# High parts of v rounded on GpSimd, PSUM banks of the MLP exchanged, weight tiles spaced evenly

## The chip, the cores and the metric

The kernel runs on one core of one Trainium2 chip. The metric is the device time of one execution in microseconds. Each comparison rests on several executions; beside them one execution is recorded by the hardware profiler, and from that one come all rows and durations below.

## The reference

Attention with pooled queries, then two MLPs, all in float32:

```python
q_pool = q.reshape(B, H, S // 2, 2, D).mean(axis=3)          # B=2, H=8, S=1152, D=64
scores = (1 / sqrt(D)) * q_pool @ k.transpose(0, 1, 3, 2)
attn = softmax(scores)                                        # with 1e-9 in the denominator
x = (attn @ v)                                                # brought to 1152 tokens x 512
h = x @ w_in;  g = where(h > 0, h, exp(min(h, 0)) - 1);  x = g @ w_out      # 512 -> 2048 -> 512
h = x @ w2_in; g = h * tanh(softplus(h));                out = g @ w2_out   # 512 -> 2048 -> 512
```

The weights of both MLPs reach the kernel as 64-bit floats, two 32-bit words each, and are brought to float32 on the chip.

## The kernel before

**Precision.** TensorE multiplies numbers of reduced precision. So each operand is split into a high part, which is the rounded number, and a low part, the number minus its high part, and each product is made of two or three matmuls (high by high, high by low, low by high). A rounding is one copy to the type fp32r, the low part is one subtraction.

**Attention.** It goes through 8 pairs of heads, n = 0 to 7, each with 9 steps of 128 query rows. A step makes scores (`scores`, L331, into a `wide` tile of two PSUM banks and a part of the `rest` bank), maxima (L338, L341, VectorE), exponentials (L353, L355, ScalarE), nine transposes (`turn`, L386), and the split of the transposed probabilities. That split is done by ScalarE and VectorE (L411, L413) or, for 13 of 27 blocks in a pair, by ScalarE and GpSimd: ScalarE copies the block from PSUM to one of two `whole` buffers (L401), GpSimd makes the high part (L201) and the low part (L202). Then come the value matmuls (`values`, L426, into `psv` banks), and `join` (L439 on ScalarE, L441 on VectorE) brings their halves together into `xf`. `finish` scales by the reciprocals R, which go through DRAM (L374, L378), on GpSimd (L449) and splits the result (L451, L453) into `xh` and `xl`, the MLP's input.

**v.** In each pair `split_v` splits v in three parts of 128 x 384: the high part (L304) and the low part on GpSimd (L306). The key `vh` (`vl`) in the table `x` sets the place of each.

**Order.** In the attention the order on each engine is written out by hand: every operation has an event time, in steps, from the table `PP['x']`, and they are issued in the order of these times. The MLP's ScalarE and VectorE work is issued in the order of the program; TensorE's and SyncE's there is not.

**Weights.** A weight tile has a number j = 2i + a in each MLP: i is the block of 128 hidden units (0 to 15), a = 0 for w_in, a = 1 for w_out. To make a tile a raw load (L554 for w_in, L557 for w_out, into one of two `raw` buffers) and a chain of operations are needed: L574 on ScalarE, then L575, L576, L577 and L579 on VectorE. The float32 tile that comes out is either split at once (`parts`: L594 on ScalarE, L596 on VectorE or GpSimd) or saved to DRAM (L601) and read back later (L549), when only the split is left. 17 tiles of the first MLP are made and saved during the attention, at the times `cs0` to `cs16`, and j = 0 and 2 are made at `fs0` and `fs1`. The list `d1` names the tiles that are not among the 17; these are made on the spot in the MLP. Those of the second MLP in `c2` are made and saved in the step of the first MLP that the entry gives.

**MLP.** For each chunk of tokens 16 steps follow. up(s) is 12 matmuls (L733) into one of four `up` banks; `elu` or `mish` then makes `gh` and `gl` (in the first MLP L692 to L696). down(s), 12 matmuls (L753) into four `acc` banks, comes three steps after up(s). So TensorE's order is up(0), up(1), up(2), up(3), down(0), up(4), down(1) and so on. The weights of up(i) are asked for two steps ahead, those of down(i) at step i + 1.

**PSUM.** There are eight banks. The attention gives the first four to `wide` (pool `ps2`) and the last four to `ps1` and `rest` (pool `ps1`). The MLP's pools take their place in the order in which they are made: `accs` the first four, `ups` the last four.

**End.** `evac` copies each `acc` bank to SBUF (L769) and sends its rows out (L776).

Of the kernel before, what the change touches and what calls it, by code (L numbers as in the profile page):

```python
# [15 lines left out]
ALU = mybir.AluOpType  # L16
AX = mybir.AxisListType
PSUM = bass.MemoryType.PSUM
# [3 lines left out]
NT = B * SQ  # L22
DM = H * D
DFF = 2048
P = 128
# [14 lines left out]

PP = {
    'ma': 'pavgs',
    'd1': [4, 7, 10, 13, 16, 22, 28, 17, 1, 27, 2, 0],
    'c2': {'1': 15, '3': 13, '5': 18, '7': 19, '9': 20, '11': 25, '13': 22, '15': 21, '17': 24, '19': 24, '21': 26, '23': 27, '25': 28, '27': 29, '29': 29, '31': 31, '30': 17, '0': 30, '24': 30, '18': 7, '12': 6, '16': 11, '22': 17},
    'L': 3,
    'ng': 4,
# [66 lines left out]
    },  # L113
}

# [2 lines left out]
class Attention:  # L118
# [180 lines left out]
    def split_v(self, n, c, part):  # L299
        nc = self.nc  # L300
        x = self.rawv[n][:, :, 3 * c:3 * c + 3, :]
        hi, lo = (self.VS[n % 2][:, :, 3 * c:3 * c + 3, i, :] for i in range(2))
        if part == 0:
            nc.scalar.copy(hi, x)  # L304
        else:
            nc.gpsimd.tensor_tensor(lo, x, hi.bitcast(F32), op=ALU.subtract)  # L306

# [307 lines left out]
def build(ctx, tc, q, k, v, w1_in, w1_out, w2_in, w2_out, out):  # L615
    nc = tc.nc
# [49 lines left out]
        if key not in W.place:  # L666
            W.place[key] = [wpa.tile([P, DM], F32R, name="w%s%d_%d" % ((x,) + key)) for x in "hl"]
    wp, gp, tmp = pool("wp", 1), pool("gp", 1), pool("mtmp", PP.get('tb', 2))
    accs, ups = pool("accs", 8 - PP['upb'], space=PSUM), pool("ups", PP['upb'], space=PSUM)
    for key in need:  # L670
        if key not in W.place:
            W.place[key] = [wp.tile([P, DM], F32R, name="w%s%d_%d" % ((x,) + key)) for x in "hl"]
# [84 lines left out]
    def evac(m, c, u):  # L757
      with prio(PP['pe']):
        ps = acc[m, c][u]
        z0, z = Z[m][c]  # L760
        if m == 0:
            h, l = (x[:, u, z0:z0 + z] for x in (xh, xl))
            nc.scalar.copy(h, ps[:, :z])
            nc.vector.tensor_tensor(l, ps[:, :z], h.bitcast(F32), op=ALU.subtract)
            if u == NCC - 1:
                fresh_to[0] = z0 + z
        else:
            o = W.wt.tile([P, DM], F32, name="wt")
            nc.scalar.copy(o[:], ps[:])  # L769
            t, end = z0 + u * P, z0 + (u + 1) * P  # L770
            while t < end:
                b, r = divmod(t, SQ)
                j, p = divmod(r, PQ)
                n = min(PQ - p, end - t)
                x = t - z0 - u * P
                nc.sync.dma_start(rows[b, j, p:p + n], o[x:x + n, :])  # L776
                t += n

    L = PP['L']
# [66 lines left out]
```

## Time and profile before

| | us |
|---|---|
| three executions | 700.38, 700.95, 696.43 |
| their median | 700.38 |
| profiled execution, its own time | 698.07 |
| its span, first to last instruction | 696.3 |

The span is what the profile's rows divide up; the 1.8 us between it and the execution's own time lie around it. Times along the axis are counted from the start of the span: the attention goes to 278 us, the first MLP from there to about 493, the second to 691, and the output to the end. An engine that is busy for nearly all of a stretch need not be what bounds it, since in the attention several are; what counts is who waits for whom.

### The profile page before, as it was taken

The page shows a single profiled execution, that of the slowest core. Times are in us where ns is not written, and L with a number is a line of the kernel's source. Part 1 is how long each engine was busy: PE and PEld are TensorE (multiplying, and loading weights), DVE is VectorE, ACT ScalarE, POOL GpSimd, SP SyncE. Part 2 cuts the span into 40 slices and gives each one's busy share as a digit, 9 for nine tenths or more (in the row PEclk, how much of TensorE's full clock was granted, in tenths as well). Part 3 has the DMA queues.
Part 4 walks back from the last instruction along what each step waited for, and adds up shares of the span by engine and source line. Part 5 has one row for each costly group of instructions (what it writes and reads, how often), then busy time and mean ns, then how long its engine had stood idle before and what let it go on. Part 6 is the DMA issues. An engine that isn't in the chain of part 4 may idle for free. (4 is left out here: it accounts for less than half of the span.)

```text
span 696.3 us, 11828 instructions
## 1 busy us (share of the span) xinstructions
PE 668.4 (96%) x3995; PEld 608.2 (87%) x3995; DVE 600.5 (86%) x1111; ACT 475.1 (68%) x1125; POOL 263.8 (38%) x308
## 2 busy tenths in 40 slices
PE   7989999999989999799999999999989999999996
PEld 4888999989989998688888999999878999999995
DVE  4889999989999998889798877786999988888884
ACT  4989999989998998575655543666655464445443
POOL 2677888878787877152220000224130000000000
PEclk7999999999999999999999999999999999999999
DMA  6785866868586530646647667565120010001001
GB/s 173 200 206 155 214 190 175 222 160 212 176 211 160 154 109 31 212 139 199 209 137 205 188 195 211 152 194 177 42 76 16 0 47 1 0 1 47 0 1 45
DMA packets 66492, 91.24 MB, mean 131 GB/s; under 512 B 24376, under 2 KB 40832, under 8 KB 66432
## 3 DMA queue, kind: packets, MB, share of 16 engines
q1 hardware_dynamic: 66432, 90.50, 46.3%
q8 instruction: 31, 0.51, 0.3%
q14 instruction: 29, 0.24, 0.1%
HBM read 60.56 MB, written 12.88 MB: 105 GB/s over the span
## 5 line engine op out<-in xcount | busy, mean ns | idle before, releaser
L733 PE MATMUL up<-xh,wh 128*128 128x384 f32 (+2 forms) x384 | 129.7, 338 | 4.2 <-DVE xf L441 4.2
L596 POOL TENSOR_TENSOR wl<-wt,wh 128x512 fp32r<-128x512 f32 x38 | 50.9, 1354 | 208.5 <-ACT wh L594 180.2
L733 PE MATMUL up<-xh,wl 128*128 128x384 f32 (+2 forms) x384 | 129.9, 338 | 0.0
L733 PE MATMUL up<-xl,wh 128*128 128x384 f32 (+2 forms) x384 | 129.5, 337 | 0.0
L202 POOL TENSOR_TENSOR tl<-whole,th 128x384 fp32r<-128x384 f32 (+1 forms) x112 | 116.5, 1040 | 9.3
L386 PE MATMUL pst<-ident,a 128*128 128x128 f32 x648 | 102.9, 278 | 5.5 <-ACT a L355 2.8
L426 PE MATMUL psv<-th,vs 128*128 128x256 f32 (+1 forms) x288 | 86.9, 322 | 0.1
L386 PEld LDWEIGHTS pst<-ident,a 128*128 128x128 f32 x648 | 74.3, 141 | 14.2 <-ACT a L355 6.1
L733 PEld LDWEIGHTS up<-xh,wh 128*128 128x128 f32 x384 | 72.8, 190 | 9.1 <-issue 4.3
L426 PE MATMUL psv<-tl,vs 128*128 128x256 f32 (+1 forms) x288 | 79.3, 295 | 0.0
L341 DVE TENSOR_REDUCE neg<-wide 128x1 f32<-128x898 f32 x72 | 78.1, 1085 | 0.8
L355 ACT ACTIVATE a<-wide,neg 128x896 f32<-128x896 f32 x72 | 74.8, 1039 | 3.4 <-DVE neg L341 3.4
L733 PEld LDWEIGHTS up<-xl,wh 128*128 128x128 f32 x384 | 72.7, 189 | 4.7
L574 ACT ACTIVATE wt<-raw 128x512 f32<-128x512 f32 x64 | 43.9, 685 | 45.7 <-DMA raw<-in_moe_w_out_dram 28.6
L201 POOL TENSOR_SCALAR th<-whole 128x384 fp32r<-128x384 f32 (+1 forms) x112 | 58.9, 526 | 42.3 <-ACT whole L401 32.3
L733 PEld LDWEIGHTS up<-xh,wl 128*128 128x128 f32 x384 | 72.6, 189 | 2.6
L413 DVE TENSOR_TENSOR tl<-pst,th 128x384 fp32r<-128x384 f32 (+1 forms) x128 | 61.1, 500 | 10.5 <-ACT th L411 9.4
L706 ACT ACTIVATE e<-n 128x384 f32<-128x384 f32 x48 | 25.2, 526 | 65.3 <-DVE n L705 65.3
L331 PE MATMUL wide<-ks,qh 128*128 128x448 f32 (+1 forms) x160 | 62.3, 403 | 5.3 <-issue 3.8
L753 PE MATMUL acc<-gl,wh 128*128 128x512 f32 (+2 forms) x192 | 64.6, 337 | 0.9 <-DVE gl L696 0.9
L753 PE MATMUL acc<-gh,wh 128*128 128x512 f32 (+2 forms) x192 | 65.1, 339 | 0.1
L753 PE MATMUL acc<-gh,wl 128*128 128x512 f32 (+2 forms) x192 | 64.4, 336 | 0.0
(95 smaller groups left out, 1670.7 us busy)
## 6 DMA issues: line engine op xcount, KB each, us to landing
raw<-in_moe_w_out_dram SPq DMA_DIRECT2D x32, 512.0 KB, 4.4
raw<-in_moe_w_in_dram SPq DMA_DIRECT2D x32, 512.0 KB, 4.3
w<-wt SPq DMA_DIRECT2D x40, 256.0 KB, 4.2
wt<-w SPq DMA_DIRECT2D x40, 256.0 KB, 3.7
kr<-in_k_dram SPq DMA_DIRECT2D x16, 288.0 KB, 4.7
vr<-in_v_dram SPq DMA_DIRECT2D x8, 576.0 KB, 3.8
qr<-in_q_dram SPq DMA_DIRECT2D x7, 576.0 KB, 5.1
qh<-tqh SPq DMA_DIRECT2D x28, 144.0 KB, 2.8
```

What stands on the lines that cost most here:

```text
L201: nc.gpsimd.tensor_scalar(hi, x, 1.0, 1.0, op0=ALU.mult, op1=ALU.mult)
L202: nc.gpsimd.tensor_tensor(lo, x, hi.bitcast(F32), op=ALU.subtract)
L331: nc.tensor.matmul(dst, w[:], x[:, cols], start=(o == 0), stop=(o == len(ops) - 1))
L341: nc.vector.tensor_reduce(neg[:], wide[:, :, :WW + 1], axis=AX.XY, op=ALU.max, negate=True)
L355: nc.scalar.activation(a[:, :2 * WW].rearrange("p (c x) -> p c x", c=2), wide[:, :, :WW], AF.Exp, bias=neg[:], accum_out=self.sums[n][:, t ...
L386: nc.tensor.transpose(ps[:, i * P:(i + 1) * P], a[:, j * P:(j + 1) * P], self.ident[:])
L413: nc.vector.tensor_tensor(l, src[:, :, x0:x0 + w], h.bitcast(F32), op=ALU.subtract)
L426: nc.tensor.matmul(ps[:, :w], self.VS[n % 2][:, h, j].rearrange("p a d -> p (a d)"), t[:, j, :w], start=(c == 1), stop=(c == 2 * NKT))
L574: lambda: nc.scalar.activation(t[:], high.bitcast(F32), AF.Abs),
L596: e.tensor_tensor(l[:], t[:], h[:].bitcast(F32), op=ALU.subtract)
L733: nc.tensor.matmul(ps[:, :z], w, x, start=(o == 0), stop=(o == len(ops) - 1))
L753: nc.tensor.matmul(ps[:, :x.shape[1]], a, x, start=(i == 0 and o == 0), stop=(i == NFF - 1 and o == 2))
```

## The change

Four things are changed.

- The high part of v is made by GpSimd, as a multiplication by 1 (twice), in place of a copy on ScalarE. Its place in the order of events is the same, now on GpSimd's list.
- The two PSUM pools of the MLP are made in the other order: `ups` takes the first four banks, `accs` the last four.
- The list `d1` of tiles made on the spot is new. Before, the tiles made on the spot in the first MLP are j = 1, 4, 7, 10, 13, 16, 17, 22, 27, 28, and 29, 30 and 31, for which no place in the attention was left. After, they are 7, 9, 11, 14, 16, 18, 20, 22, 24, 26, 28, 30 and 31. Both are 13. The other 17 are made in the attention. The times of `cs4` and `cs16` are exchanged, so the tile that is made last there is j = 29 (before: j = 9); both are w_out tiles.
- The last output tile is copied in two halves, by ScalarE and VectorE, and the last of its two output transfers is issued by ScalarE.

The entry `isq` of the table only stands elsewhere in it.

```diff
-    'd1': [4, 7, 10, 13, 16, 22, 28, 17, 1, 27, 2, 0],
+    'd1': [7, 9, 11, 14, 16, 18, 20, 22, 24, 26, 28, 30, 31],
...
-        'cs2': 26.9397, 'cs3': 3.684, 'cs4': 76.2237, 'cs5': 22.2118, 'cs6': 35.9869, 'cs7': 9.0113, 'cs8': 49.2134, 'cs9': 58.2337, 'cs10': 44.9952,
-        'cs11': 31.1952, 'cs12': 62.3751, 'cs13': 7.9386, 'cs14': 40.1687, 'cs15': 13.2473, 'cs16': 53.9176, 'fs0': 66.983, 'fs1': 72.9632,
+        'cs2': 26.9397, 'cs3': 3.684, 'cs4': 53.9176, 'cs5': 22.2118, 'cs6': 35.9869, 'cs7': 9.0113, 'cs8': 49.2134, 'cs9': 58.2337, 'cs10': 44.9952,
+        'cs11': 31.1952, 'cs12': 62.3751, 'cs13': 7.9386, 'cs14': 40.1687, 'cs15': 13.2473, 'cs16': 76.2237, 'fs0': 66.983, 'fs1': 72.9632,
...
         hi, lo = (self.VS[n % 2][:, :, 3 * c:3 * c + 3, i, :] for i in range(2))
         if part == 0:
-            nc.scalar.copy(hi, x)
+            nc.gpsimd.tensor_scalar(hi, x, 1.0, 1.0, op0=ALU.mult, op1=ALU.mult)
         else:
             nc.gpsimd.tensor_tensor(lo, x, hi.bitcast(F32), op=ALU.subtract)
...
-    accs, ups = pool("accs", 8 - PP['upb'], space=PSUM), pool("ups", PP['upb'], space=PSUM)
+    ups, accs = pool("ups", PP['upb'], space=PSUM), pool("accs", 8 - PP['upb'], space=PSUM)
...
             o = W.wt.tile([P, DM], F32, name="wt")
-            nc.scalar.copy(o[:], ps[:])
+            last = z0 + (u + 1) * P == NT
+            if last:
+                nc.scalar.copy(o[:, :DM // 2], ps[:, :DM // 2])
+                nc.vector.tensor_copy(o[:, DM // 2:], ps[:, DM // 2:])
+            else:
+                nc.scalar.copy(o[:], ps[:])
...
-                nc.sync.dma_start(rows[b, j, p:p + n], o[x:x + n, :])
+                (nc.scalar if last and end - t == n else nc.sync).dma_start(rows[b, j, p:p + n], o[x:x + n, :])
```

## Rows read from the trace of the kernel before

**Rows 1.** The page, part 2: granted TensorE clock in 40 slices, in tenths.

```profile
PEclk7999999999999999999999999999999999999999
```

**Rows 2.** Stages: length, busy us (instructions) of PE PEld DVE ACT POOL, clock, DMA.

```profile
36.00:270.00 234.00, 224.64 (x1618) 210.63 (x1617) 219.46 (x396) 219.38 (x580) 189.39 (x232) 1.00 0.66 173
...
278.30:282.60 4.30, 0.14 (x2) 0.03 (x1) 4.11 (x9) 1.30 (x3) 0.00 (x0) 1.00 0.47 138
282.60:286.20 3.60, 3.60 (x9) 2.81 (x10) 2.46 (x3) 0.87 (x2) 1.43 (x1) 0.56 0.98 333
...
312.00:332.00 20.00, 20.00 (x90) 16.57 (x89) 18.28 (x31) 11.83 (x23) 4.54 (x3) 1.00 0.62 197
```

**Rows 3.** Timeline of TensorE from attention to MLP: start, duration, line, [idle before <-releaser].

```profile
278.16 0.28 PE L426 MATMUL psv<-tl,vs 128*128 128x256 f32 x1
282.60 0.47 PE L733 MATMUL up<-xh,wh 128*128 128x512 f32 x1 [4.16 <-DVE xf L441]
...
295.19 0.39 PE L753 MATMUL acc<-gh,wh 128*128 128x512 f32 x1
```

**Rows 4.** Timeline of VectorE and ScalarE in the same stretch.

```profile
282.49 0.69 DVE L596 TENSOR_TENSOR wl<-wt,wh 128x512 fp32r<-128x512 f32 x1
283.56 0.69 ACT L574 ACTIVATE wt<-raw 128x512 f32<-128x512 f32 x1 [3.69 <-DMA raw<-in_moe_w_in_dram]
293.25 0.68 DVE L696 TENSOR_TENSOR gl<-up,gh 128x512 fp32r<-128x512 f32 x1
```

**Rows 5.** Timeline of TensorE at the start of a pair's scores.

```profile
143.48 0.47 PE L331 MATMUL wide<-ks,qh 128*128 128x448 f32 x1 [1.51 <-DMA ks<-kl]
```

**Rows 6.** Line L549, read-back of saved tiles: issue to landing.

```profile
DMA to landing us min/median/max: 2.5/3.7/5.4
```

**Rows 7.** Groups by line, 36 to 270 us: busy us, mean ns | idle before.

```profile
L201 POOL TENSOR_SCALAR th<-whole 128x384 fp32r<-128x384 f32 x87 | 47.6, 547 | 25.9 <-ACT whole L401 16.0 <-ACT row L372 8.2 <-PE pst L386 1.4
L413 DVE TENSOR_TENSOR tl<-pst,th 128x384 fp32r<-128x384 f32 x87 | 46.3, 550 | 6.7 <-ACT th L411 5.8
L331 PE MATMUL wide<-ks,qh 128*128 128x448 f32 x72 | 30.3, 436 | 5.3 <-issue 3.8 <-DMA ks<-kl 1.5
L304 ACT CAST vs<-vr 128x384 fp32r<-128x384 f32 x19 | 10.6, 559 | 0.0
```

**Rows 8.** Timeline of ScalarE and VectorE in a pair without a wait for keys.

```profile
106.78 0.59 ACT L304 CAST vs<-vr 128x384 fp32r<-128x384 f32 x1
107.78 1.02 DVE L413 TENSOR_TENSOR tl<-pst,th 128x384 fp32r<-128x384 f32 x2 [0.41 <-ACT th L411]
```

**Rows 9.** Timeline of GpSimd and ScalarE in the same pair.

```profile
103.20 0.35 POOL L201 TENSOR_SCALAR th<-whole 128x192 fp32r<-128x192 f32 x1 [1.31 <-ACT whole L401]
110.39 1.37 POOL L202 TENSOR_TENSOR tl<-whole,th 128x384 fp32r<-128x384 f32 x1
112.22 0.49 ACT L401 COPY whole<-pst 128x384 f32<-128x384 f32 x1
```

**Rows 10.** Timeline of VectorE: one operation without and with GpSimd at work.

```profile
291.00 0.42 DVE L575 TENSOR_SCALAR wt<-wt 128x512 f32<-128x512 f32 x1
301.87 1.05 DVE L575 TENSOR_SCALAR wt<-wt 128x512 f32<-128x512 f32 x1
```

**Rows 11.** Timeline of ScalarE, VectorE and TensorE in steps 6 to 9.

```profile
316.53 0.67 ACT L574 ACTIVATE wt<-raw 128x512 f32<-128x512 f32 x1 [2.71 <-DMA raw<-in_moe_w_out_dram]
321.03 0.66 ACT L574 ACTIVATE wt<-raw 128x512 f32<-128x512 f32 x1 [3.32 <-DMA raw<-in_moe_w_in_dram]
321.73 0.43 DVE L575 TENSOR_SCALAR wt<-wt 128x512 f32<-128x512 f32 x1 [1.04 <-ACT wt L574]
323.98 0.68 DVE L696 TENSOR_TENSOR gl<-up,gh 128x512 fp32r<-128x512 f32 x1
327.83 0.39 PE L753 MATMUL acc<-gh,wh 128*128 128x512 f32 x1
```

**Rows 12.** Timeline of SyncE at the end: six issues.

```profile
690.25 3.08 SPq L776 DMA_DIRECT2D out_dram<-wt  x6
```

42 rows, old and new, of the table PP are left out of this document.

## The prediction

> **What bounds the kernel now.** I read the page first, then busy time by stage, then the single stages along the time axis, then the groups of instructions. The page shows TensorE at the full clock in all 40 slices but the first [rows 1]. The stages show what slices of 17 us hide [rows 2]. From 36 to 270 us, the steady attention, TensorE, VectorE and ScalarE are all at 94 to 96% and GpSimd at 81% (189.4 of 234): three engines share the bound there. In the MLP (312 to 332) TensorE never pauses, 90 matmuls in 20.0 us, so there only a late operand costs time. [...] The rows of the hole name its end: the last attention matmul starts at 278.16, the first up-matmul at 282.60 after a wait for the xf addition of VectorE (L441), the last reader of an attention bank [rows 3]. The first down-matmul, down(0), starts at 295.19. Four up steps of 12 matmuls lie before it; at some 0.226 us each (20.0/90 = 0.222, a little more as the window's edges cut matmuls) that is 10.9 us, so of the 16.9 us from 278.3 to 295.2 some 6.0 are lost: 4.3 idle and about 1.7 by the slow clock.
>
> **Banks exchanged.** After the change the up tiles lie where the score tiles lay. These are last read by the exponentials, before the last transposes and value matmuls of the attention, so up(0) may follow the value matmuls at 278.3 at once. What is late next is the weights. For j=2 (up(1)) the low part is the subtraction at 282.49, done at 283.18 [rows 4]; VectorE works without a pause up to it, so it doesn't come sooner. up(1) needs it in its third matmul, at 278.3 + 14 x 0.226 = 281.5: a wait of 1.7 us. In the attention TensorE waits 1.51 us at one place [rows 5] in a stretch whose clock stays at 1.00 [rows 2], so I count no slow stretch behind it. Tile j=4 (up(2), due at 283.2 + 10 x 0.226 = 285.5) is no longer made on the spot, where its first step waited 3.69 us for a load and ran at 283.56 [rows 4]; it is read back, 3.7 us from issue to landing [rows 6]. Issued at about 279.3, in the place of the load that it replaces, it lands at 283 and is split by 284.5: in time. Tile j=1 likewise. down(0) also needs gl(0), which came at 293.25 + 0.68 because two made-on-the-spot chains stood before it on ScalarE and VectorE [rows 4]; both are gone, and by 290.9 it is there. So down(0) starts at 278.3 + 10.9 + 1.7 = 290.9 instead of 295.2: a gain of 4.3 us. Bounds: 6.0 if nothing is late, 0 if something holds down(0) until 295. As TensorE has no pause in the stretch behind it, the gain stays.
>
> **v on GpSimd.** 24 casts (8 pairs, 3 parts) of 559 ns leave ScalarE, 13.4 us, and 24 operations like the 547 ns of L201 come to GpSimd, 13.1 us [rows 7]; the trace has no such operation on v itself, but L201 has its shape and form. GpSimd goes from 81 to about 86% in the steady stretch. Bounds: a gain of 13.4 us if ScalarE alone set the pace, a loss of 13.1 if GpSimd did. The nearest rows lie close to neither. Behind the cast at 106.78, VectorE waits 0.41 us for ScalarE [rows 8]; that wait can go. But GpSimd works without a pause from 103.20 past 112, and the split that ends at 110.39 + 1.37 = 111.76 frees the buffer that ScalarE fills at 112.22, 0.46 us later [rows 9]. Two new operations fall into this stretch, 1.1 us, so that copy would wait about 0.64 us, with the exponentials and casts of ScalarE queued behind it, and VectorE, which has no slack there, behind these. In the pairs where TensorE waits before the scores (L331, 5.3 us in the stretch, the longest for the keys' DMA [rows 5, 7]), that wait covers GpSimd's delay, and the gain on ScalarE is mostly swallowed by it too. I count +0.4 us in each of three pairs without that wait and -0.3 in four with it: 0 in sum. At the start nothing moves: the three casts of the first pair follow the parts that the first scores need.
>
> The other side of the edit is VectorE. The same operation on SBUF alone, L575, takes 0.42 us with GpSimd idle and 1.05 with it at work [rows 10]. GpSimd's busy share rises by 13.1/234 = 5.6%, so only that share of VectorE's SBUF-only work meets it anew, and most of VectorE's attention work reads PSUM; under 1 us, counted at nothing. [...]
>
> **Weight tiles.** Thirteen tiles are made on the spot before and after. Before, they start at j=4 and 1, in the hole; after, the first is j=7, and j=7, 14, 9, 16, 11 and 18, with two tiles of the second MLP (c2 entries 12 and 18), fall to steps 4 to 7: 8 chains where there were 5. Each chain is about 2.25 us of VectorE (321.73 to 323.98) and holds one of two load buffers, and ScalarE stands still until its load has landed: 3.32 us at 321.03, with four chains in steps 6 and 7. The gl(6) that this delays is done at 323.98 + 0.68; its down starts at 327.83, so 3.2 us of slack were left [rows 11]. In the new order step 6 has three chains, the third loaded only when the first has freed its buffer. By the same rows (one chain per 4.5 us, 316.53 to 321.03 on ScalarE) the high parts of j=16 and 18 come within a us of their ups. I count a loss of 1.0 us; bounds 0 (the slack of 3.2 holds) and 8 (8 chains x 4.5 = 36 us against four steps of 24 x 0.226 = 5.4 and some 6 us of slack). Exchanging cs4 and cs16 keeps the tile that is saved last a w_out tile, so nothing moves.
>
> **The end.** Six output DMAs are issued on SyncE in 3.08 us, 0.51 each [rows 12]. Now one is issued by ScalarE beside SyncE's five, after two half copies: the last issue on SyncE ends 0.5 us sooner. Gain 0.5.
>
> **Sum.** -4.3 + 0 + 1.0 - 0.5 = -3.8. Against the profiled execution's own 698.07 (span 696.3, 1.8 around it): 694.3. The three runs have their median at 700.38, 2.3 above; the middle of all four is 699.2, and the forecast on it is 695.4, 0.7% under the median.
>
> **Rivals.** (1) ScalarE held the attention back and GpSimd isn't late: VectorE's waits for the casts, 5.8 us at L413 [rows 7], go: 689.6. Against: VectorE is as full as ScalarE. Chance 0.25. (2) The exchange brings nothing forward, as read-back tiles land late or down(0) is held otherwise: the 4.3 go, 699.7. For it: all read-backs share SyncE with the transfer of R; chance 0.15. (3) Bunched weight tiles stall TensorE in steps 7 to 10 by the bound of 8 us: 702.4. For it: ScalarE's standing in rows 11; against: the slack of 3.2 us there. 0.17. (4) The other side: GpSimd becomes the bound of the attention. It decides once GpSimd's stretch outlasts its idle time in each pair, and each new operation then costs its full 0.55: 695.4 + 13.1 = 708.5, slower. Against: 1.31 us of idle time ahead of the stretch [rows 9], and 19% overall. 0.08. (5) Each new operation blocks one of VectorE's SBUF-only ones: 24 x 0.63 = 15.1, 710.5. Against: these are a small part of its work, and GpSimd meets them now. 0.04. The forecast keeps 0.31, its own range being 692 to 699.
>
> **Chances.** About 1% is what a measurement of this kernel can tell from no change: 693.4 and 707.4. Faster: most of (1), 0.21, and a quarter of the forecast, 0.08. Slower: most of (4), (5) and a worse (3), 0.09. The rest, 0.62, is within 1%. The range, 688 to 703, takes in the forecast, (2), (3) and (1) with up to 1.6 us more; (4), (5) and the far ends of (1) and (3) are left out.
>
> **What would show it.** First up-matmul within 0.3 us of the last value matmul, no clock under 0.9 in the 4 us after, one wait of about 1.7 us in up(1), down(0) 12 to 13 us after the last value matmul. In the attention: the time from pair to pair unchanged within 0.5 us; ScalarE waiting for GpSimd at L401 by 0.5 us and more in some pairs. In steps 8 to 10, ups that wait up to 1 us for wl. The prediction is wrong if the attention's end moves by over 3 us, if down(0) still starts 16 us after it, or if the waits in the MLP sum to over 6 us more than now.

## The result, and the profile after

The changed kernel is slower by 0.67%: a ratio of 1.0067 to the kernel before, with a 95% interval of 1.0043 to 1.0090 (medians 703.49 and 699.23 us of runs on the same chip). That is within the 1% of the forecast's middle class, but the forecast was 0.7% faster, and 703.5 lies just above its range. The profiled execution took 703.30 us with a span of 701.26, to be set beside 698.07 and 696.28.

Four times cut both spans into stages: the last value matmul, down(0), the first up of the second MLP, and the end of the last matmul.

| Stage | before, us | after, us | difference |
|---|---|---|---|
| start to last value matmul (attention) | 278.16 | 282.79 | +4.6 |
| to down(0) (transition) | 17.03 | 12.49 | -4.5 |
| to the first up of the second MLP | 187.12 | 192.64 | +5.5 |
| to the end of the last matmul | 208.65 | 208.59 | -0.1 |
| to the end of the span | 5.32 | 4.75 | -0.6 |

So the gain at the transition came as forecast, and two losses hid it. The transition first, in the timeline of TensorE (columns as in [rows 3]):

```profile
282.79 0.28 PE L426 MATMUL psv<-tl,vs 128*128 128x256 f32 x1
282.91 0.39 PE L733 MATMUL up<-xh,wh 128*128 128x512 f32 x1
...
286.16 0.39 PE L733 MATMUL up<-xh,wh 128*128 128x512 f32 x1
...
287.87 0.50 PE L733 MATMUL up<-xh,wl 128*128 128x512 f32 x1 [1.09 <-DVE wl L596]
...
295.28 0.39 PE L753 MATMUL acc<-gh,wh 128*128 128x512 f32 x1
```

The wait of 4.16 us for the attention's last VectorE operation [rows 3], the hole from 278.3 to 282.6 us, is gone: the first up-matmul follows at once. One wait is left, 1.09 us for the low part of j=2. The forecast had 1.7 us at the third matmul of up(1). In this kernel TensorE does two more matmuls with high parts first (the third starts at 286.16), so only the fifth waits; the low part itself is as late as forecast (287.87 less 286.16 is 1.7). The stages, with the columns of [rows 2], show that the clock no longer falls there (1.00 from 282.9 to 287.5 us, where 0.56 was granted behind the hole [rows 2]), what the steady attention looks like, and the new hole in the MLP:

```profile
36.00:270.00 234.00, 221.28 (x1582) 205.93 (x1581) 216.10 (x387) 209.46 (x549) 194.55 (x245) 1.00 0.66 173
282.90:287.50 4.60, 3.88 (x18) 2.75 (x16) 4.41 (x9) 3.34 (x7) 0.00 (x0) 1.00 0.67 233
...
316.00:336.00 20.00, 16.94 (x71) 12.66 (x70) 16.72 (x28) 12.26 (x23) 4.28 (x3) 1.00 0.69 205
```

In 20 us of the MLP TensorE does 71 matmuls where it did 90 [rows 2]. What it waits for from the transition into the second MLP, in the list of waits (engine, tile and line, releaser: us in total, times, longest):

```profile
PE up L733 <- DVE wl L596: 3.5, 3, 1.4
PE acc L753 <- ACT gh L712: 1.7, 1, 1.7
PE up L733 <- ACT wh L594: 1.3, 2, 1.1
PE acc L753 <- DVE xl L764: 1.0, 2, 0.6
PE up L733 <- POOL wl L596: 0.6, 1, 0.6
```

The three lines of "up" are new. Apart from the 1.09 us at up(1), which the first of them holds, they are weight tiles that come late at up(8), up(9) and up(15). Read as lengthened distances from one matmul to the next, the places of over 0.3 us in that stage sum to 5.8 us here (0.4 to 1.5 each) and to 1.0 in the kernel before. The line with gh, in the second MLP, is in the kernel before too, at the same 1.7 us.

In the attention, ScalarE is freed as meant, from 219.4 to 209.5 us in the steady stretch, and GpSimd goes from 189.4 to 194.6. The groups by line and shape (columns of [rows 7]) show the price of the cast in its new place; the last fence has the narrower shape of L413 in the kernel before:

```profile
L413 DVE TENSOR_TENSOR tl<-pst,th 128x384 fp32r<-128x384 f32 x84 | 44.9, 546 | 6.6 <-ACT th L411 6.2
...
L304 POOL TENSOR_SCALAR vs<-vr 128x384 fp32r<-128x384 f32 x19 | 14.6, 768 | 0.0
L413 DVE TENSOR_TENSOR tl<-pst,th 128x192 fp32r<-128x192 f32 x28 | 8.6, 352 | 2.6 <-ACT th L411 2.5
```

```profile
L413 DVE TENSOR_TENSOR tl<-pst,th 128x192 fp32r<-128x192 f32 x28 | 8.6, 351 | 1.1 <-ACT th L411 1.0
```

A cast of v takes 768 ns on GpSimd in this stretch, not the 547 that the forecast took from L201. VectorE's wait for ScalarE's casts at L413, which was to shrink, is 6.2 us where it was 5.8 [rows 7], and for the narrower shape 2.5 where it was 1.0. The timeline shows how, in the pair that answers to [rows 8, 9]:

```profile
111.70 0.72 DVE L579 SCALAR_TENSOR_TENSOR wt<-raw,wt 128x512 int32<-128x512 int32 x1
111.84 0.95 POOL L304 TENSOR_SCALAR vs<-vr 128x384 fp32r<-128x384 f32 x1
113.35 1.01 POOL L202 TENSOR_TENSOR tl<-whole,th 128x384 fp32r<-128x384 f32 x1
114.40 0.48 ACT L401 COPY whole<-pst 128x384 f32<-128x384 f32 x1 [0.49 <-POOL tl L202]
115.75 0.56 DVE L413 TENSOR_TENSOR tl<-pst,th 128x384 fp32r<-128x384 f32 x1 [0.48 <-ACT th L411]
```

The cast at 111.84 lasts 0.95 us, beside VectorE's L579. The split behind it ends at 114.36 and only then may ScalarE refill the buffer `whole`: it waited 0.49 us, with the exponentials queued behind, and VectorE's next subtraction waited 0.48.

### The profile page after: what moved, and what is told of

The parts are those of the page before. It is cut to its first block, busy times and chain, and to the rows that moved or that the text cites. A ratio compares the mean times of both kernels' runs of the same rounds, so it can differ in the third digit from the quotient of the medians.

```text
span 701.3 us, 11837 instructions
## 1 busy us (share of the span) xinstructions
PE 670.4 (96%) x3995; PEld 606.7 (87%) x3995; DVE 604.6 (86%) x1112; ACT 467.3 (67%) x1101; POOL 275.0 (39%) x332
## 5 line engine op out<-in xcount | busy, mean ns | idle before, releaser
L201 POOL TENSOR_SCALAR th<-whole 128x384 fp32r<-128x384 f32 (+1 forms) x112 | 58.3, 521 | 38.1 <-ACT whole L401 30.6
L413 DVE TENSOR_TENSOR tl<-pst,th 128x384 fp32r<-128x384 f32 (+1 forms) x128 | 61.2, 498 | 11.7 <-ACT th L411 11.2
```

Of the source, the lines that this page charges most:

```text
L201: nc.gpsimd.tensor_scalar(hi, x, 1.0, 1.0, op0=ALU.mult, op1=ALU.mult)
L413: nc.vector.tensor_tensor(l, src[:, :, x0:x0 + w], h.bitcast(F32), op=ALU.subtract)
```

## Each part alone

The first four runs undo or do one part at a time. In the edits below the kernel before is the base unless something else is said.

**v alone.**

```diff
-            nc.scalar.copy(hi, x)
+            nc.gpsimd.tensor_scalar(hi, x, 1.0, 1.0, op0=ALU.mult, op1=ALU.mult)
```

> The kernel before with one edit: the high parts of v on GpSimd. Theory A (ScalarE's copies into the buffers `whole` wait for GpSimd): the attention alone loses what it lost in the changed kernel, its last value matmul at about 282.8 instead of 278.2, pairs that don't wait for the keys' DMA 32.4 us apart instead of 31.5, and the time is 4 to 5 us over the kernel before (about 703.5). Rival B (the other order of the saved weight tiles, which also run through the attention, did it): last value matmul within 0.7 us of 278.2, no difference in time.

**Banks alone.**

```diff
-    accs, ups = pool("accs", 8 - PP['upb'], space=PSUM), pool("ups", PP['upb'], space=PSUM)
+    ups, accs = pool("ups", PP['upb'], space=PSUM), pool("accs", 8 - PP['upb'], space=PSUM)
```

> The kernel before with one edit: the PSUM banks of the MLP exchanged, the weight tiles as before (j=4 and j=1 still made on the spot in the hole). Theory C (the exchange and the tiles are worth their 4.5 us only together): up(0) follows the last value matmul at once, but up(2) waits for j=4 and down(0) for gl(0), which stand behind two made-on-the-spot chains; down(0) starts 14 to 16 us after the last value matmul instead of 17.0, a gain of 1 to 3 us. Rival D (the banks alone bring the gain): down(0) 12.5 us after it, gain 4.5 us, 694.7.

**Tiles alone.**

```diff
-    'd1': [4, 7, 10, 13, 16, 22, 28, 17, 1, 27, 2, 0],
+    'd1': [7, 9, 11, 14, 16, 18, 20, 22, 24, 26, 28, 30, 31],
-        'cs4': 76.2237, ... 'cs16': 53.9176
+        'cs4': 53.9176, ... 'cs16': 76.2237
```

> The kernel before with one edit: the list of the tiles made on the spot (and cs4 with cs16 exchanged). Theory E (the bunching in steps 4 to 7 is what stalls TensorE): the stalls of steps 8 to 16, 5.5 us in the changed kernel, are there in full although nothing brings TensorE forward; time up by 4 to 5 us. Rival F (the stalls are the gain of the transition handed back, the chains can't follow a TensorE that is 4.5 us earlier): stalls under 2 us, and the time within 2 us of the kernel before.

**All but v.** The changed kernel with `nc.scalar.copy(hi, x)` back in its place.

> The changed kernel with one edit undone: the high parts of v are back on ScalarE; banks, tiles and the end as changed. By theory A the attention ends at 278.2 as in the kernel before, down(0) starts 12.5 us later at 290.7, the stalls of steps 8 to 16 stay at about 5.5 us, and the time is 0 to 1 us over the kernel before (699 to 700), 4.6 under the changed one. By rival B the attention still ends at 282.8 and the time is that of the changed kernel (703.5).

| Run | ratio to before (95%) | attention ends | down(0) after it | first up of the second MLP after it |
|---|---|---|---|---|
| before | | 278.2 | 17.0 | 204.2 |
| changed | 1.0067 (1.0043 to 1.0090) | 282.8 | 12.5 | 205.1 |
| v alone | 1.0046 (1.0022 to 1.0069) | 282.0 | 17.0 | 203.1 |
| banks alone | 1.0004 (0.9984 to 1.0024) | 276.1 | 17.8 | 203.3 |
| tiles alone | 1.0094 (1.0071 to 1.0118) | 277.0 | 17.7 | 211.0 |
| all but v | 1.0018 (0.9988 to 1.0048) | 280.6 | 12.5 | 205.0 |

The end of the attention differs from execution to execution (275.0 to 280.9 us in the twelve profiled executions with v on ScalarE, as the waits for transfers at the start of the pairs differ), so one trace doesn't price v; the timed ratios and the pairs do. The 280.6 of all but v, for one, holds a wait of 2.67 us for the keys and a clock of 0.57 in the 4 us behind it.

*v alone* costs 0.46%, 3.2 us, less than the 4 to 5 of theory A, but where it said: the weight tiles have no part in the attention's loss. From the first scores of a pair to those of the next, the third and fourth pair, which don't wait for the keys, take 32.45 and 32.55 us instead of 31.51 and 31.60. The last pair takes 38.87 us from its first scores to the last value matmul instead of 37.82, and in the twelve executions with v on ScalarE this is 37.77 to 37.83.

*Banks alone* bring nothing. Rival D falls; theory C had the reason, but its gain of 1 to 3 us didn't come. up(0) starts at once, but up(1) waits 1.54 us and up(2) 2.71, the latter for j=4, which is still made on the spot, and behind that the clock is down, so that down(0) comes 17.8 us after the attention:

```profile
281.19 0.50 PE L733 MATMUL up<-xh,wl 128*128 128x512 f32 x1 [1.54 <-DVE wl L596]
...
286.46 0.50 PE L733 MATMUL up<-xh,wh 128*128 128x512 f32 x1 [2.71 <-ACT wh L594]
```

```profile
281.20:283.60 2.40, 2.40 (x10) 1.78 (x10) 1.25 (x2) 1.78 (x3) 1.08 (x1) 1.00 0.92 292
286.40:290.00 3.60, 3.54 (x11) 2.50 (x12) 3.46 (x7) 2.61 (x6) 0.00 (x0) 0.74 0.75 247
290.00:294.00 4.00, 4.00 (x16) 3.27 (x15) 3.18 (x5) 3.26 (x7) 2.04 (x2) 0.80 0.72 239
```

(The second fence has stages around the two waits; the clock is the third number from the end: 1.00, 0.74, 0.80.) *Tiles alone* cost 0.94%, 6.6 us (theory E had 4 to 5), though nothing brings TensorE forward, and the same late tiles stand in its list of waits:

```profile
PE up L733 <- DVE wl L596: 2.5, 2, 1.6
PE up L733 <- ACT wh L594: 1.2, 2, 0.8
PE up L733 <- POOL wl L596: 0.6, 1, 0.6
```

So theory E holds against F: the stalls belong to the list. Banks and tiles are worth their gain only together: 0.3 and 6.6 us alone, 1.3 together (with the halved last output), 5.6 less than their sum. And v's 3.2 and the 1.3 make 4.5 of the measured 4.7 us.

## Where v's loss comes from

If it is the place in GpSimd's order, another place must mend it. In the run with v alone GpSimd was idle for 0.9 us just before buffer 14 of each pair, and busy without a pause from there to the last part of v.

```diff
-        'vh0': 7.0318, ... 'vh2': 6.5211,
+        'vh0': 5.31, ... 'vh2': 5.3,
```

> The kernel before with v on GpSimd, and the casts of two of its three parts (vh0 and vh2) moved to an earlier place of GpSimd's order, before the `whole` buffer number 14 of a pair, where the run with v on GpSimd shows GpSimd idle for 0.9 us. Theory A (the place matters: the casts lie in the stretch in which GpSimd has no pause, and make ScalarE's copies wait for it at L401): the pairs, less the waits for the keys, are 31.4 to 31.7 us apart again and the last pair 37.8 instead of 38.9; the time is 2.5 to 3.5 us under that run, within 1 us of the kernel before. [...]

The ratio is 1.0008 (0.9978 to 1.0037), no loss that can be told from zero. Its interval still overlaps that of v alone (1.0022 to 1.0069) a little, so the times by themselves don't settle it. The traces do, for theory A: the last pair takes 37.93 us, where casts that cost the same at any place would have left it at the 38.87 of v alone. The two traces at the same place, the turn from pair 6 to pair 7 (GpSimd, VectorE and ScalarE), first with v at its old place, then early:

```profile
240.17 0.51 POOL L304 TENSOR_SCALAR vs<-vr 128x384 fp32r<-128x384 f32 x1
243.06 0.73 DVE L579 SCALAR_TENSOR_TENSOR wt<-raw,wt 128x512 int32<-128x512 int32 x1
243.18 0.98 POOL L304 TENSOR_SCALAR vs<-vr 128x384 fp32r<-128x384 f32 x1
245.79 0.48 ACT L401 COPY whole<-pst 128x384 f32<-128x384 f32 x1 [0.52 <-POOL tl L202]
```

```profile
230.92 1.20 POOL L304 TENSOR_SCALAR vs<-vr 128x384 fp32r<-128x384 f32 x2
240.87 0.49 ACT L401 COPY whole<-pst 128x384 f32<-128x384 f32 x1
```

At the old place the two casts take 0.51 and 0.98 us out of a stretch that had none to give, and the copy of ScalarE waits 0.52 for GpSimd (GpSimd's next operations start 0.47 and 0.95 us after the two casts, which bears their lengths out); early, both lie ahead of the stretch (1.20 us together) and the copy doesn't wait. From the first scores of pair 7 to those of its third step it is 7.07 us before, 8.13 with v at its old place and 7.20 with v early (238.88 to 246.08). The scores of the kernel before and of v at its old place:

```profile
240.34 0.45 PE L331 MATMUL wide<-ks,qh 128*128 128x448 f32 x1
...
247.41 0.45 PE L331 MATMUL wide<-ks,qh 128*128 128x448 f32 x1
```

```profile
243.16 0.45 PE L331 MATMUL wide<-ks,qh 128*128 128x448 f32 x1
...
251.29 0.45 PE L331 MATMUL wide<-ks,qh 128*128 128x448 f32 x1
```

Note that the early place gains nothing over ScalarE either: 13.4 us less work on ScalarE bring nothing that these times show.

## What paces the weight tiles

The next runs keep the banks and the halved last output, leave v on ScalarE and change where chains stand. First a list spread more evenly, with j=4 and j=1 still kept out of the transition (by this list six chains fall to steps 4 to 7, not the seven of the expectation):

```diff
-    'd1': [7, 9, 11, 14, 16, 18, 20, 22, 24, 26, 28, 30, 31],
+    'd1': [7, 10, 13, 14, 16, 17, 20, 24, 27, 28, 29, 30, 31, 2, 0],
```

> The kernel before with the banks exchanged, the last output in two halves, and a list of tiles made on the spot that keeps j=4 and j=1 out of the transition like the changed kernel's, but has at most two chains (second-MLP tiles counted) in one of the steps 4 to 7, 7 in all instead of 8, and none of the pairs 14 with 9, 16 with 11; v on ScalarE. Theory E (the tiles' stalls come from the bunch): down(0) 12.5 us after the last value matmul, stalls of steps 8 to 16 under 1.5 us instead of 5.5, time 4 to 5 us under the kernel before (0.6 to 0.7%). Rival H (a TensorE that comes 4.5 us earlier runs into late tiles with any list): stalls of 4 us and more, time that of the kernel before.

Then the changed list, with two tiles of the second MLP moved out of steps 6 and 7:

```diff
-    'c2': { ... '18': 7, '12': 6, ...
+    'c2': { ... '18': 16, '12': 23, ...
```

> The changed kernel with v back on ScalarE and two second-MLP tiles (c2 entries 12 and 18) moved from steps 6 and 7 to steps 23 and 16; the list of tiles made on the spot as changed. Theory E (eight chains through two load buffers in steps 4 to 7 are too many; six are not): the waits before up(8) and up(9), 2.2 and 1.7 us, fall to under 1 us together, and the time is 3 us or more under the same kernel with the two left in place (697). Rival I (the list of first-MLP tiles alone is too dense, one in each step from 4 to 13 and two in 5 and 6): the waits stay above 2.5 us together, the time falls by less than 1.5 us.

The ratios are 1.0032 (1.0006 to 1.0057) and 1.0016 (0.9998 to 1.0033): no gain in either, though both traces show the early stalls gone, but for 0.7 us at up(10) in the first (which the later expectations call up(9)) and 0.4 in the second. In the first run, then, theory E was right on the early stalls and rival H on the time. In place of those stalls TensorE stands at the change from the first pass to the second (the first MLP takes the tokens in three passes of 16 steps each), 3.04 us in the first run and 4.27 in the second, before down(16), whose PSUM tiles must first be emptied by ScalarE and VectorE. The timeline of ScalarE and TensorE in the first run says why:

```profile
374.64 0.66 ACT L574 ACTIVATE wt<-raw 128x512 f32<-128x512 f32 x1 [2.70 <-DMA raw<-in_moe_w_in_dram]
378.69 0.67 ACT L574 ACTIVATE wt<-raw 128x512 f32<-128x512 f32 x1 [2.21 <-DMA raw<-in_moe_w_out_dram]
380.41 2.04 ACT L763 CAST xh<-acc 128x512 fp32r<-128x512 f32 x4
382.38 0.56 PE L753 MATMUL acc<-gh,wh 128*128 128x384 f32 x1 [3.04 <-DVE xl L764]
```

ScalarE's copies out of PSUM (380.41) stand in its order behind the first operation of a chain, and that waits for its load. Counted from the last value matmul, this operation starts at 98.2 us in the kernel before, at 97.8 here and at 98.4 in the second run: the loads come at their own pace, whatever TensorE does, so a TensorE that is 4.5 us earlier waits there for what it had gained.

If so, fewer loads ahead of that place should free it. Five second-MLP tiles were put off, with the spread list, with the changed list, and with the spread list and v at the early place:

```diff
-    'c2': { ... '18': 7, '12': 6, '16': 11, '22': 17, '30': 17, ...
+    'c2': { ... '18': 34, '12': 32, '16': 33, '22': 36, '30': 40, ...
```

> The kernel with exchanged banks, halved last output and the spread list, and five second-MLP tiles (c2 entries 12, 16, 18, 22, 30) saved late, in steps 32 to 40 instead of 6 to 17; v on ScalarE. Theory H2 (the loads of the chains run at a pace of their own, one per 3.6 us from about 70 us after the attention on, and ScalarE stands behind them; a TensorE that is 4.5 us earlier meets them 4.5 us too early at the change from the first to the second pass): with 18 us of loads taken out before step 20 the stall of 3.2 us at down(16) and that of 0.7 at up(9) go, and the time is 3 to 4 us under the same kernel with the old c2 list, 2 to 4 us under the kernel before. Rival J (the stall at the change of pass comes from the evacuation alone, four copies by ScalarE and VectorE that an earlier TensorE doesn't wait less for): it stays at 3 us, and no time is gained.

> The changed kernel with v back on ScalarE, its list of tiles made on the spot kept, and the same five second-MLP tiles saved late. Theory H2: the waits before up(8), up(9) and up(15), 2.2, 1.7 and 1.5 us, and the 4.4 us at down(16) that came when two tiles were only moved to steps 16 and 23, are all under 1 us; time 4 to 5 us under the changed kernel with v on ScalarE (695 where the kernel before takes 697 to 699). Rival I (the list itself is too dense): over 2.5 us of the waits stay in steps 8 to 16.

> The first kernel of this set and v on GpSimd with vh0 and vh2 at the early place. By theory A, as the early place cost and gained nothing when it stood alone, the time is that of the first kernel of this set within 1 us; if ScalarE, freed of 13.4 us, now lets the pairs follow closer, 1 to 3 us less.

The early stalls went as theory H2 had it: from down(0) to down(30), the last but one of the second pass, there is no stall of over 0.4 us in any of the three, the changed list's 5.5 us gone among them. The times did not follow: 1.0158 (1.0120 to 1.0195), 1.0153 (1.0115 to 1.0192) and 1.0184 (1.0148 to 1.0220). The five tiles are now missed later; in the first of them:

```profile
PE acc L753 <- DVE xl L764: 4.9, 1, 4.9
PE acc L753 <- DVE gl L696: 4.8, 3, 1.8
```

The 4.9 us are the change to the third pass. The second MLP takes longer too, 211.3 to 211.6 us in the three instead of 208.65. The run with v early doesn't differ from its twin by more than the intervals, so it says no more on v. A milder move, three tiles (22 to step 23, 30 to 40, 24 to 43) with the spread list:

> The kernel with exchanged banks, halved last output and the spread list, v on ScalarE, and three second-MLP tiles of c2 moved: 22 from step 17 to 23, 30 from 17 to 40, 24 from 30 to 43, where the runs show the chains of the weight tiles 6 to 8 us apart instead of 3.6. Theory H2 (the chains' loads have a pace of their own; TensorE keeps the 4.5 us of the transition only where the chains ahead of each change of pass are thinned by as much, and the late steps can take three chains but not five): no stall over 1 us at down(16) (3.2 with the old places) nor at the change to the third pass (5.0 with five tiles late, 1.0 before); time 4 to 5.5 us under the kernel before (ratio 0.992 to 0.995). Rival K (the chains are at their limit in the whole first MLP, whatever is moved comes back as a stall elsewhere): stalls of 4 us and more in sum, ratio 0.998 to 1.004.

1.0058 (1.0036 to 1.0081). Both changes of pass were free of stalls, and 3.5 us of waits turned up in the third pass instead, with 1.5 and 0.9 more than before at two places of the second MLP. For two load buffers rival K had the mechanism: what is moved comes back as a stall elsewhere. The ratio is even above the 0.998 to 1.004 that it gave.

That left open what makes the pace. A third buffer for the loads tells:

```diff
+            self.k += 1
-            t = self.rawp.tile([P, 2 * DM], I32, name="raw")
+            t = (self.rawx if self.rawx and self.k % 3 == 0 else self.rawp).tile([P, 2 * DM], I32, name="raw")
...
+    W.rawx = pool("wraw2", 1)
-        e, n, p = (tmp.tile([P, ZM if x == "e" else max(PP['z2'])], F32, name=x)[:, :h.shape[1]] for x in "enp")
+        e, n, p = (tmp.tile([P, ZM if x == "e" else max(PP['z2'])], F32, name=x, bufs=2 if x == "e" else 1)[:, :h.shape[1]] for x in "enp")
```

with the changed list, with the spread list, and on the kernel before. These lines move the later ones, so in the three runs a line of the chains has a number higher by two (L577 to L581 are L575 to L579 of the other kernels), and one of the MLP a number higher by three:

> The changed kernel with v back on ScalarE, and a third buffer for the weight tiles' loads in the MLP (every third load goes to it; the space comes from the tiles n and p of the second MLP's activation, one instead of two each). Theory L (a pair of load buffers sets the chains' pace, and ScalarE stands before a load that was issued late for want of a buffer): ScalarE's waits for landings in the first MLP, 42 us in the changed kernel, fall by more than half, and the waits before up(8), up(9) and up(15), 5.5 us, to under 1.5 us; the first MLP is 4 to 5 us shorter. Rival M (the transfers themselves, or VectorE's four operations on each tile, set the pace): with a third buffer the loads only land later after their issue, ScalarE's waits fall by less than a quarter and over 4 us of the stalls stay. In the second MLP the single n and p may cost some us either way.

> The kernel with exchanged banks, halved last output and the spread list (old c2 list, v on ScalarE) with the third load buffer. Theory L: the stall of 3.2 us at down(16) goes, that of 0.7 at up(9) too, and the 4.5 us of the transition are kept up to the second MLP: from the last value matmul to the last down of the first MLP 4 us less than in the kernel before. Rival M: the stall at down(16) stays within 1 us of its 3.2.

> The kernel before with the third load buffer alone, n and p of the second MLP single. It gives the price of the single n and p in the second MLP for the two others. By theory L it gains only the 1.0 us that the first MLP of the kernel before loses at the change to the third pass, as its weight tiles are otherwise in time; by rival M nothing.

| Run with a third load buffer | ratio to before (95%) | down(0) after the attention | first up of the second MLP after it | ScalarE waits for loads, 283 to 445 us |
|---|---|---|---|---|
| changed list | 1.0001 (0.9972 to 1.0030) | 12.5 | 202.9 (205.0 with two) | 8.3 us (41.1 with two) |
| spread list | 0.9957 (0.9929 to 0.9984) | 12.8 | 199.8 (205.1) | 7.0 us (39.3) |
| kernel before | 0.9987 (0.9961 to 1.0012) | 18.3 | 203.0 (204.2) | 6.5 us (45.4) |

ScalarE's standing before the loads is gone in all three. The time of a load from issue to landing is 3.9 us (median) with two buffers and with three, so the loads were not slow: they were issued late, for want of a buffer. With the spread list theory L holds. The stall at down(16) falls from 3.04 to 0.7 us, the gain of the transition is kept up to the second MLP (199.8 against 204.2), and the kernel is the only one here that beats the one before, by 0.43%, though the single n and p cost it 0.7 us in the second MLP (209.3 us from its first up to the last matmul, 208.65 before):

```profile
PE up L736 <- DVE wl L598: 1.1, 1, 1.1
PE acc L756 <- DVE xl L767: 0.7, 1, 0.7
PE up L736 <- POOL wl L598: 0.6, 1, 0.6
```

(These are all its waits from the transition to 440 us.) With the changed list theory L fails: 5.1 us of stalls stay, 3.1 of them at up(9). There a second limit lies right behind the first. VectorE, in the 25 us in which the chains of steps 4 to 7 run, with the columns of [rows 2], and the two engines side by side:

```profile
302.00:327.00 25.00, 22.20 (x97) 17.76 (x96) 24.21 (x38) 13.70 (x25) 5.78 (x4) 1.00 0.59 171
```

```profile
314.49 2.99 POOL L598 TENSOR_TENSOR wl<-wt,wh 128x512 fp32r<-128x512 f32 x2 [5.19 <-ACT wh L596]
314.59 1.74 DVE L579 SCALAR_TENSOR_TENSOR wt<-raw,wt 128x512 int32<-128x512 int32 x1
316.37 1.66 DVE L581 SCALAR_TENSOR_TENSOR wt<-raw,wt 128x512 int32<-128x512 int32 x1
```

VectorE is at work for 24.21 of 25 us, and the stalls that stay are for low parts that it makes (3.7 us of waits at up for L598 on VectorE, apart from up(1)). An estimate of its work in steps 4 to 7: eight chains of 2.25 us, four steps with two operations of 0.69 each, and 2.0 us by which L579 and L581 are stretched beside GpSimd's subtractions (1.74 and 1.66 instead of 0.69) make 25.5 us, without the low parts, against 21.7 for four steps of TensorE (24 x 0.226 each). With two buffers VectorE wasn't yet the limit there: in the changed kernel it works 20.73 us of the 25 from 304 us on. A further buffer doesn't mend the second limit; with the spread list, which has fewer chains there, all but the waits in the fence above are gone (VectorE at 23.25 us of 25 from 299 us on, TensorE at work throughout). That VectorE is the second limit is read from these rows and the estimate; no run changes its work alone.

## Why the prediction was wrong

**Banks exchanged: right.** First up 0.12 us after the last value matmul, one wait (1.09 us for a forecast 1.7, as TensorE puts two other matmuls ahead), clock at 1.00, down(0) 12.5 us after the attention for a forecast 12.6. The gain of the transition was 4.5, forecast 4.3. One sentence of this part failed: "As TensorE has no pause in the stretch behind it, the gain stays." TensorE had no pause, but the chains beside it had no slack either; with two load buffers no list and no placement tried kept the gain.

**v on GpSimd: right in mechanism and place, mis-sized.** The sum had 0; it was 3.2 us. The path was the forecast's: two new operations ahead of a copy with 0.46 us of slack [rows 9]. What failed are the sizes. The casts took 0.51 and 0.98 us where both were counted at 0.55, so the same subtraction gives 1.03 us instead of 0.64. The sum then took only 0.4 for each of the three pairs without a wait for the keys, and these lost 0.94, 0.95 and 1.05. And the -0.3 for each of the four pairs with that wait isn't in the traces: with v alone they differ from the kernel before by +1.2, 0.0, +0.2 and -0.7 us, as the wait for the keys itself differs, and the early place, too, frees ScalarE of 13.4 us and gains nothing. The bound of a loss of 13.1 held, and of the two signs the row with 0.46 us of slack had the right one.

**Weight tiles: the largest miss.** Forecast 1.0, measured 6.6 alone and 5.5 in the changed kernel's stage from down(0) to the second MLP. The step that failed is the slack. The sum had the high parts of j=16 and j=18 "within a us of their ups", and "3.2 us of slack were left" is that of a gl. In the changed kernel TensorE lost 2.1 us to j=16 and 1.7 to j=18, at up(8) and up(9), and 1.5 to j=30 at up(15), which the sum doesn't have at all. It had the two load buffers and ScalarE's standing, but not VectorE's own time in steps 4 to 7 (an estimated 25.5 against 21.7 us), the limit right behind. The bound of 8 held. Rival 3, bunched tiles at 702.4 us, was the nearest of all to the result, at a chance of 0.17.

**The end: 0.6, forecast 0.5** in the changed kernel's trace; the five issues left on SyncE take 2.63 us where six took 3.08 [rows 12]. But that it came to 0.6 is in part luck: of the ten traces with this edit, the stage behind the last matmul takes 4.74 and 4.75 us in two (the spread list's and this one) and 5.14 to 5.26 in eight, against 5.28 to 5.35 in the six without it. What makes the difference between them stays open.

With the terms as measured the sum is -4.5 + 3.2 + 5.5 - 0.6 = +3.6, or about 701.7 on the profiled execution's own 698.07; the rest of its 703.30 is for the most part the attention's spread from execution to execution (it is 4.6 us longer in these two traces, and v costs 3.2 in the timed runs). The chances for (1) and (4) fell as the forecast argued: ScalarE was no bound, and the loss per cast (3.2/24 = 0.13) stayed far under the full 0.55. Rival 5 was right that the two engines get in each other's way, and wrong on who waits: beside L579 it was the cast on GpSimd that took 0.95 to 0.98 us instead of 0.50 to 0.52.

## What to carry to other kernels

Before you count a gain upstream as kept, look at the producers beside the bound engine: an engine whose next operation waits at each load for a buffer keeps its own time (with two buffers ScalarE came to the change of pass 97.8 to 98.4 us after the attention, with TensorE 4.5 us earlier or not), and a faster consumer only waits for it at the next place where both meet. When work is moved between steps, sum each engine's work in the steps that receive it, not only the slack of one result. A cast moved to a less busy engine costs by the moment at which it runs there (0.51 us or up to 0.98 for the same cast of v); look for a place where that engine is idle, and at what the other engines run beside it, before you look at its average share.

## What the runs showed of the hardware

The same cast of v took 0.50 to 0.52 us on GpSimd in 12 of 24 cases of the run with v alone and 0.95 to 0.98 in eleven (one took 0.77). Each of the eleven began while VectorE ran the last operation of a chain (L579), which reads two operands from SBUF, and each of the 12 ran beside operations that read PSUM. The other way round, the last two operations of a chain (L579 and L581 of the run with a third buffer) took 1.74 and 1.66 us instead of 0.69 on VectorE beside GpSimd's subtraction. In the eleven casts and in the L579 of that run (GpSimd's subtractions begin at 314.49 us, L579 at 314.59) the longer time stands in the record of the instruction that began second, not as a wait before it.

From 20 us on, the clock was 1.00 in the 4 us behind each of the 18 waits of TensorE of 0.6 to 1.94 us in the traces of the kernel before and the changed kernel, and in the 2.4 us behind the 1.54 of the run with the banks alone. It was lower behind these longer ones: 0.57 in the 4 us after the 2.67 of the run with all but v, 0.74 in the 3.6 us after the 2.71 of the banks alone, 0.56 after 4.16 [rows 2, 3], and 0.50 in the four us after the 4.27 of the run with two chains moved (clock third from the end):

```profile
378.00:382.00 4.00, 3.85 (x12) 3.85 (x13) 3.93 (x9) 2.40 (x6) 0.00 (x0) 0.50 0.78 222
382.00:386.00 4.00, 4.00 (x21) 4.00 (x20) 3.86 (x8) 1.45 (x4) 0.00 (x0) 0.83 0.47 106
```

The length of a wait alone doesn't give the clock behind it. The clock is 1.00 behind a wait of 2.07 us (third buffer with the changed list, up(9)) and 0.59 behind one of 1.76 (spread list with five tiles late, down(31)):

```profile
325.60:329.60 4.00, 4.00 (x18) 3.29 (x19) 3.90 (x8) 1.71 (x3) 0.00 (x0) 1.00 0.81 257
```

```profile
435.90:439.90 4.00, 4.00 (x16) 4.00 (x17) 3.90 (x7) 1.05 (x5) 1.29 (x1) 0.59 0.65 196
```
